# A spectral layer with an MLP behind it on one Trainium2 core: the second product two steps behind, eight places for the kept half, earlier reads, no preferred work

## Chip, cores and metric

The kernel runs on one core of a Trainium2 chip. The metric is the device time of one execution in microseconds (us), the median of several runs. All arrays are float32.

## What is computed

```
X  = rfft(x, axis=1)                       # x: 8 x 3008 x 256
Yr = Xr @ w_r - Xi @ w_i + b_r             # w_r, w_i: 256 x 256
Yi = Xr @ w_i + Xi @ w_r + b_i
Y  = sign(Y) * max(|Y| - 0.01, 0)          # real and imaginary part apart
y  = irfft(Y, n=3008, axis=1)
h  = y.reshape(24064, 256) @ w_in          # w_in: 256 x 2048, float64 in memory
out = max(0.01 * h, h) @ w_out             # w_out: 2048 x 256, float64 in memory
```

## The kernel before

Two pieces of work share TensorE. The **transform** of one batch element is cut as 3008 = 47 x 64: `fwd` (L229) does the 47-point stage, `mid` (L325) the 64-point stage (`stage_b`, L351), the projection (`proj`, L384), the threshold and the 64-point stage back (`stage_g`, L423), and `inverse` (L480) the 47-point stage back. The **MLP** goes over 32 chunks of 752 tokens. In `moe` (L639) a chunk has two phases.

- *Phase one* has eight steps, q = 0 to 7. A step makes 256 of the 2048 hidden features by seven block products in place of eight: `moe_a` (L553) issues four of them into the four `psh` banks, `moe_b` (L575 and the lines above it) three more onto three of these banks. Each product is three matmuls of 376 columns, since every operand is split into a high and a low part (`block`, L91, L98). Between the two groups VectorE and ScalarE must take sums out of the banks: L560 on ScalarE copies the first bank into `p1`, L561 to L563 on VectorE add the others. After the second group L575 and L577 (ScalarE, leaky ReLU) and L576 (VectorE) finish one token half, `gf`, and L580 (VectorE) with L584 (ScalarE) the other, `gs`, which is kept in SBUF until phase two. `parts` (L589) splits a half into its operands: `gh` by a copy on ScalarE (L594), `gl` by a subtraction on VectorE (L595). They rotate through six `gg` places, that is three pairs.
- The *second product*, `moe_o` (L602, matmuls on L612), adds a step's `gf` to two `pso` banks. In phase one it is issued in two groups of six matmuls, one behind `moe_a`, one behind `moe_b`, and takes the oldest entry of the list `behind`: the step before the present one.
- *Phase two* runs `moe_o` over the eight kept halves, 12 matmuls each. `late` (L598) splits a kept half; two are split in the last two steps of phase one, the others behind each group of phase two. `forms` (L508) makes the next chunk's operands meanwhile.

Transform work of the next batch element is traced between the groups. What order it gets is set by a scheduler: a list of ready instructions per engine, earliest traced first, with modelled times. `tc.issue_after` ties MLP matmuls to the order in which they are traced. `tc.high_priority(AHEAD)` (L560 to L563, L575 to L580) lets the instructions in it go ahead of up to 200 others.

The prologue (0 to about 145 us) reads and converts the weights and transforms the first batch element. `load_wout` (L192) reads w_out in eight pieces; the first `next(wout)` issues two of them behind `m0.finish()`. Two lines more are spoken of: the input tiles of the second batch element (`fwd(1)`) take the places that `XT` (L228) gives, the last pair that of `yc`, and `turns(0)` (L433) reads the first 64-point matrix.

Of the kernel before, what the change touches and what calls it, by code (L numbers as in the profile page):

```python
# [8 lines left out]
F32 = mybir.dt.float32  # L9
F32R = mybir.dt.float32r  # L10
U32 = mybir.dt.uint32
# [8 lines left out]
NG, NS = 5, 13  # L20
# [10 lines left out]
def spectral_mlp_kernel(  # L31
# [98 lines left out]
    def load_weights():  # L130

        w = early[:, 6 * D:6 * D + 3 * NH * D + P]
        r, d, n = (w[:, k * NH * D:(k + 1) * NH * D].rearrange("p (a f) -> p a f", a=NH) for k in range(3))
        i = sb.tile([P, NH, D], F32, name="w_i", tag="yt", bufs=1)
# [20 lines left out]
    made, converted, parted, early_parts = [], [], [], []  # L155
    AHEAD = 200

# [33 lines left out]
    def load_wout():  # L191
# [5 lines left out]
        def load():  # L197
            k = len(raws)
            raw = sb.tile([P, CS, 2], U32, name="raw", tag="ez"[k % 2], bufs=1)
            with tc.issue_after(reads[-1].ins):  # L200
                sync.dma_start(raw.rearrange("p (a f) w -> p a (f w)", a=n), ov[:, k * n:(k + 1) * n, :])
            raws.append(raw)
# [24 lines left out]
    NX = -(-NS // 2)  # L227
    XT = [("gs", NQ - 1)] * 2 + [("gg", 6)] * 3 + [("gs", NQ - 1), ("yc", 3)]  # L228

    def fwd(b):  # L230
# [5 lines left out]
        def load(c):  # L236
            cols = slice(2 * c * D, min(2 * c + 2, NS) * D)
            n = cols.stop - cols.start
            if b < NPRE:
                tag, bufs = XT[c]  # L240
                x_t[c] = [sb.tile([PA, 2 * D], F32, name="xin", tag=tag, bufs=bufs)[:, :n] for h in range(2)]
            else:
                x_t[c] = [
                    sb.tile([PA, 2 * D], F32, name=f"xin{h}", tag="uv"[h], bufs=3 - h)[:, :n] for h in range(2)
                ]
            for h, t in enumerate(x_t[c]):
                if b == 0:
# [76 lines left out]

    def mid(b):  # L325
        ud = u_dram[b]
        vd = dram.tile([2, NK1, NG * NS, D], F32, name="v_dram", tag="v_dram")
# [3 lines left out]
        act.dma_start(vd.rearrange("c k n d -> (c k) n d")[:, N2, :], zero)  # L331
        u_t, e_t, z_t, fb_t = {}, {}, {}, {}
        if b == 0:
# [4 lines left out]
        def load(j):  # L338
# [5 lines left out]
            u_t[j] = u  # L344

        def turns(j):
            if j < NPAIR:
                fb_t[j] = sb.tile([P, 3, N2], F32, name="fb", tag="fb")
                sync.dma_start(fb_t[j], fb[j])

# [27 lines left out]
        def proj(j):  # L378
# [4 lines left out]
            for dst, c, w in ((0, 2, "wr"), (0, 1, "wn"), (D, 0, "wd")):  # L383
# [5 lines left out]
                if c == 2:  # L389
                    kc = sb.tile([P, D], F32, name="kc", tag="kc", bufs=1)  # L390
# [8 lines left out]
            t = sb.tile([P, 2, D], F32, name="t", tag="t" if b else "v", bufs=1 if b else 2)  # L399
            c = sb.tile([P, 2, D], F32, name="c", tag="kb" if b else "yt", bufs=1)  # L400
            dve.tensor_add(flat(t), ps_y, flat(kb))  # L401
# [30 lines left out]

        turns(0)  # L433
        for j in range(2):
# [45 lines left out]
    def inverse(pi, eh):  # L480
# [11 lines left out]
        odd = sb.tile([P, 2 * NG * NK1], F32, name="odd", tag="odd", bufs=1)[:, :ne]  # L492
        y = sb.tile([P, CS], F32, name="y", tag="y")
        act.copy(odd, py[:, ne:2 * ne])
# [12 lines left out]
    def forms(ci):  # L507
# [3 lines left out]
        b11, b21, b12, b22 = y0[:, 0], y0[:, 1], y1[:, 0], y1[:, 1]  # L511
        t = sb.tile([P, 2, HT], F32, name="yt", tag="yt", bufs=1)
        y2 = sb.tile([P, 2, 7, 2, HP], F32R, name="yhl", tag="yhl", bufs=1)
# [11 lines left out]
        yield  # L525
        dve.tensor_sub(t[:, 1], b22, t[:, 0])
        dve.tensor_sub(b12, b22, b12)
        yield
        split(slice(2, 4), t)
        yield  # L530
        split(slice(4, 6), y1)
        dve.tensor_sub(b11, b21, t[:, 1])
        yield
# [15 lines left out]
    def moe_a(ci, q):  # L549
# [5 lines left out]
        product(c12, ci, q, 5, True)  # L555
        u = sb.tile([P, HT], F32, name="p1", tag="p1")
        g1 = sb.tile([P, 2, 2, HP], F32, name="gs", tag="gs", bufs=NQ - 1)
        g = g1[:, :, :, :HH]
        with tc.high_priority(AHEAD):
            act.copy(u, c11[:, :HT])  # L560
            dve.tensor_add(u, c22[:, :HT], u)  # L561
            dve.tensor_add(g[:, 1], halves(c21[:, :HT]), halves(u))  # L562
            dve.tensor_add(g[:, 1], halves(c12[:, :HT]), g[:, 1])  # L563
        h_t[ci, q] = (c11, c21, c12, u, g1)

    def moe_b(ci, q):
# [6 lines left out]
        g = g0[:, :, :, :HH]  # L573
        with tc.high_priority(AHEAD):
            act.activation(g[:, 0], halves(c11[:, :HT]), AF.Prelu, alpha=SLOPE)  # L575
            dve.tensor_add(g[:, 1], halves(c21[:, :HT]), halves(u))  # L576
            act.activation(g[:, 1], g[:, 1], AF.Prelu, alpha=SLOPE)  # L577
            parts(ci, q, 0, g0)
            g = g1[:, :, :, :HH]
            dve.tensor_add(g[:, 0], halves(c12[:, :HT]), halves(u))  # L580
        early_parts[:] = parted
# [57 lines left out]
    def moe():  # L639

        behind = []

        def next_o(eh):
            if behind:
                in_order(moe_o, *behind[0], eh)
                if eh:
                    behind.pop(0)

        for ci in range(nch):
            nxt = tokens(ci + 1) if ci + 1 < nch else iter(())  # L650
            units = 0
            for q in range(NQ):
# [8 lines left out]
                next(nxt, None)  # L661
                if q >= NQ - 2:
                    late(ci, q + 2 - NQ)
                units += 15
# [3 lines left out]
            nxt = forms(ci + 1) if ci + 1 < nch else iter(())  # L668
            behind += [(ci, q, 1) for q in range(NQ)]
            for q in range(NQ):  # L670
                for eh in range(NH):
                    next_o(eh)
                    if eh:
                        late(ci, q + 2)
                    with tc.issue_after(early_parts[0].ins), tc.issue_after(early_parts[1].ins):
# [3 lines left out]
        while behind:  # L679
            for eh in range(NH):  # L680
                next_o(eh)

# [27 lines left out]
    f0.to(0.01)  # L710
    load_win(0, (sync, act))
    load_weights()
    sign = const.tile([P, NK1 + NPAIR], F32, name="sign")
# [10 lines left out]
    with tc.issue_after(turned[0].ins):  # L724
        split_consts()
    m0 = Stream(mid(0), MID)
    m0.to(0.001)
# [12 lines left out]
    for i in range(1, 17):  # L740
# [3 lines left out]
        if 5 <= i < 12:  # L744
            next(fp.gen)
    m0.finish()
    fp.to(0.69)
    for p in due[0]:
        v_load(p)
    next(wout)  # L750
    for eh in range(NH):
# [143 lines left out]
```

## Time and profile before

| | |
|---|---|
| runs | 2581.2, 2583.67, 2587.37 us; median 2583.67 |
| profiled execution | 2589.46 us, its span 2587.7 us |
| TensorE (PE) busy / weight loads (PEld) busy | 2455.0 / 2336.0 us |
| VectorE (DVE) / ScalarE (ACT) / GpSimd (POOL) busy | 1891.2 / 1658.8 / 248.0 us |
| granted TensorE clock | 0.987 of 2.4 GHz |
| DMA | 173.68 MB, 67 GB/s on average |

The engines' queues run in order. A row of waits tells who stood idle, on which tile and line, and whose instruction ended the wait. In a timeline row the number in brackets is the idle time just before. "PE" rows are matmuls, whose ends are modelled, "PEld" rows weight loads, which run ahead of them. L-numbers are lines of the kernel before; in the order of the changed kernel they are those of the changed file.

### The profile page before, as it was taken

The numbers are of one execution on the slowest core, as the hardware profiler recorded it, in microseconds if no ns is written. First come the engines' busy times: TensorE is split into PE (matmuls) and PEld (weight loads), VectorE is DVE, ScalarE is ACT, GpSimd is POOL, SyncE is SP. The second block draws the span as 40 slices with busy tenths as digits, with TensorE's granted clock in tenths as the row PEclk, the third lists the DMA queues.
The fourth block names the chain that finished last, engine by engine and source line by source line (L and its number), as shares of the span: only waits on it lengthen the run. The fifth ranks groups of instructions, "written<-read, shape, count | busy, mean of one in ns | idle before, by whom it ended". The sixth has DMA issues, their size and how long they took to land.

```text
span 2587.7 us, 41422 instructions
## 1 busy us (share of the span) xinstructions
PE 2455.0 (95%) x15388; PEld 2336.0 (90%) x15388; DVE 1891.2 (73%) x3208; ACT 1658.8 (64%) x3198; POOL 248.0 (10%) x192
## 2 busy tenths in 40 slices
PE   6879999999999999999999999999999999999999
PEld 4569999999899998999989999899999999999998
DVE  6687788677776777777777767777768777766665
ACT  4666676667566666676656766566766666655554
POOL 0200012000110001100011001100002000000000
PEclk8989999999999999999999999999999999999999
DMA  7531123221231212321123211321213221100000
GB/s 234 164 119 54 49 56 114 71 57 51 71 95 53 57 45 76 86 66 49 49 81 86 57 53 44 93 79 51 60 50 100 65 59 40 44 28 28 17 13 19
DMA packets 138479, 173.68 MB, mean 67 GB/s; under 512 B 15661, under 2 KB 100645, under 8 KB 138277
## 3 DMA queue, kind: packets, MB, share of 16 engines
q1 hardware_dynamic: 97688, 124.17, 16.0%
q10 hardware_dynamic: 40589, 46.87, 7.1%
q8 instruction: 121, 1.98, 0.3%
q14 instruction: 81, 0.66, 0.1%
HBM read 95.22 MB, written 75.76 MB: 66 GB/s over the span
## 4 chain that ended last, share of the span: by engine, by line
PE 70%; DVE 12%; ACT 11%; DMA 3%; issue 2%; POOL 0%; SPq 0%; ACTq 0%; DVEq 0%; POOLq 0%
PE pso L612 30%; PE psh L98 25%; PE psf L82 10%; PE psf L491 3%; DVE gl L595 2%; ACT gh L594 2%; ACT zf L411 2%; PE psf L359 1%; ACT gf L577 1%; DVE t L403 1%; ACT zf L407 1%; DVE gs L562 1%; DVE t L401 1%; DVE p L561 1%; DVE gf L576 1%
## 5 line engine op out<-in xcount | busy, mean ns | idle before, releaser
L98 PE MATMUL psh<-yhl,win_hi 128*128 128x376 f32 x3584 | 884.0, 329 | 15.7 <-DVE gs L562 8.5
L98 PEld LDWEIGHTS psh<-yhl,win_hi 128*128 128x128 f32 x3584 | 610.8, 190 | 40.8 <-DVE gs L562 15.8
L98 PE MATMUL psh<-yhl,win_lo 128*128 128x376 f32 x1792 | 578.5, 323 | 0.0
L612 PE MATMUL pso<-gl,wout_hi 128*128 128x376 f32 x2048 | 505.1, 328 | 15.4 <-DVE gl L595 14.1
L612 PE MATMUL pso<-gh,wout_hi 128*128 128x376 f32 x2048 | 502.7, 327 | 15.4 <-ACT gh L594 15.2
L612 PE MATMUL pso<-gh,wout_lo 128*128 128x376 f32 x2048 | 496.7, 324 | 0.0
L612 PEld LDWEIGHTS pso<-gl,wout_hi 128*128 128x128 f32 x2048 | 353.0, 190 | 32.3 <-DVE gl L595 30.2
L612 PEld LDWEIGHTS pso<-gh,wout_hi 128*128 128x128 f32 x2048 | 353.6, 190 | 30.3 <-ACT gh L594 25.6
L612 PEld LDWEIGHTS pso<-gh,wout_lo 128*128 128x128 f32 x2048 | 359.1, 190 | 0.0
L98 PEld LDWEIGHTS psh<-yhl,win_lo 128*128 128x128 f32 x1792 | 339.0, 189 | 0.2 <-issue 0.2
L595 DVE TENSOR_TENSOR gl<-gf,gh 128x752 fp32r<-128x752 f32 x256 | 245.9, 961 | 106.8 <-ACT gh L594 104.5
L595 DVE TENSOR_TENSOR gl<-gs,gh 128x752 fp32r<-128x752 f32 x256 | 242.4, 958 | 63.8 <-ACT gh L594 63.6
L393 POOL TENSOR_TENSOR kb<-bias,kc 128x512 f32<-128x512 f32 x96 | 133.6, 1392 | 1613.5 <-ACT kc L391 1577.7
L594 ACT CAST gh<-gs 128x752 fp32r<-128x752 f32 x256 | 209.9, 822 | 111.4 <-PE pso L612 100.3
L575 ACT ACTIVATE gf<-psh 128x376 f32<-128x376 f32 x256 | 124.3, 485 | 234.0 <-PE psh L98 188.3
L561 DVE TENSOR_TENSOR p<-psh,p 128x376 f32<-128x376 f32 x256 | 140.1, 547 | 137.4 <-ACT p L560 121.4
L577 ACT ACTIVATE gf<-gf 128x376 f32<-128x376 f32 x256 | 132.6, 518 | 140.9 <-DVE gf L576 138.0
L576 DVE TENSOR_TENSOR gf<-psh,p 128x376 f32<-128x376 f32 x256 | 139.6, 545 | 112.7 <-PE psh L98 111.8
L594 ACT CAST gh<-gf 128x752 fp32r<-128x752 f32 x256 | 209.8, 820 | 6.2
L584 ACT ACTIVATE gs<-gs 128x752 f32<-128x752 f32 x256 | 212.1, 828 | 1.5 <-DVE gs L580 0.7
L560 ACT COPY p<-psh 128x376 f32<-128x376 f32 x256 | 117.8, 460 | 98.6 <-PE psh L98 98.4
L580 DVE TENSOR_TENSOR gs<-psh,p 128x376 f32<-128x376 f32 x256 | 139.5, 545 | 20.0 <-PE psh L98 17.7
(130 smaller groups left out, 3538.5 us busy)
## 6 DMA issues: line engine op xcount, KB each, us to landing
u<-u_dram SPq DMA_DIRECT2D x192, 128.0 KB, 2.8
v_dram<-v ACTq DMA_DIRECT2D x192, 128.0 KB, 2.4
out_dram<-ob SPq DMA_DIRECT2D x128, 188.0 KB, 1.9
vin<-v_dram SPq DMA_DIRECT2D x94, 240.0 KB, 3.4
xin<-x_dram SPq DMA_DIRECT2D x90, 240.0 KB, 3.0
u_dram<-xin ACTq DMA_DIRECT2D x72, 240.0 KB, 2.4
fb<-fb_dram SPq DMA_DIRECT2D x96, 96.0 KB, 2.0
u_dram<-xin SPq DMA_DIRECT2D x24, 240.0 KB, 3.9
```

What stands on the lines that cost most here:

```text
L82: last = nc.tensor.matmul(dst, a, b, start=(i == 0), stop=(i == len(terms) - 1))
L98: mlp[:] = [nc.tensor.matmul(dst, a, b, start=start and i == 0, stop=i == 2, skip_group_check=True)]
L393: pool.tensor_add(kb, bias, kc.unsqueeze(1).broadcast_to([P, 2, D]))
L561: dve.tensor_add(u, c22[:, :HT], u)
L575: act.activation(g[:, 0], halves(c11[:, :HT]), AF.Prelu, alpha=SLOPE)
L576: dve.tensor_add(g[:, 1], halves(c21[:, :HT]), halves(u))
L577: act.activation(g[:, 1], g[:, 1], AF.Prelu, alpha=SLOPE)
L580: dve.tensor_add(g[:, 0], halves(c12[:, :HT]), halves(u))
L584: act.activation(g, g, AF.Prelu, alpha=SLOPE)
L594: cp = act.copy(h, g)
L595: parted[:] = [cp, dve.tensor_sub(l, g, h.bitcast(F32))]
L612: mlp[:] = [nc.tensor.matmul(pv, a[:, f, s], turned_halves(r[:, i]), start=(f == 0 and j == 0), stop=(f == NF - 1 and j == 2),)]
```

## The change

Five edits, cut to the lines that matter:

```diff
 def moe():
-        def next_o(eh):
-            if behind:
+        def next_o(eh, least=2):
+            if len(behind) >= least:
                 in_order(moe_o, *behind[0], eh)
...
                 behind.append((ci, q, 0))
                 next(nxt, None)
-                if q >= NQ - 2:
-                    late(ci, q + 2 - NQ)
...
             behind += [(ci, q, 1) for q in range(NQ)]
+            late(ci, 0)
             for q in range(NQ):
                 for eh in range(NH):
                     next_o(eh)
                     if eh:
-                        late(ci, q + 2)
+                        late(ci, q + 1)
...
-        u = sb.tile([P, HT], F32, name="p1", tag="p1")
-        g1 = sb.tile([P, 2, 2, HP], F32, name="gs", tag="gs", bufs=NQ - 1)
+        u = sb.tile([P, HT], F32, name="p1", tag="p1", bufs=1)
+        g1 = sb.tile([P, 2, 2, HP], F32, name="gs", tag="gs", bufs=NQ)
-        with tc.high_priority(AHEAD):
-            act.copy(u, c11[:, :HT])
...
+        act.copy(u, c11[:, :HT])
...
-        with tc.high_priority(AHEAD):
-            act.activation(g[:, 0], halves(c11[:, :HT]), AF.Prelu, alpha=SLOPE)
-            dve.tensor_add(g[:, 1], halves(c21[:, :HT]), halves(u))
-            act.activation(g[:, 1], g[:, 1], AF.Prelu, alpha=SLOPE)
-            parts(ci, q, 0, g0)
-            g = g1[:, :, :, :HH]
-            dve.tensor_add(g[:, 0], halves(c12[:, :HT]), halves(u))
+        act.activation(g[:, 0], halves(c11[:, :HT]), AF.Prelu, alpha=SLOPE)
+        dve.tensor_add(g[:, 1], halves(c21[:, :HT]), halves(u))
+        act.activation(g[:, 1], g[:, 1], AF.Prelu, alpha=SLOPE)
+        g = g1[:, :, :, :HH]
+        dve.tensor_add(g[:, 0], halves(c12[:, :HT]), halves(u))
+        parts(ci, q, 0, g0)
...
 def forms(ci):
-        t = sb.tile([P, 2, HT], F32, name="yt", tag="yt", bufs=1)
+        t = sb.tile([P, 1, HT], F32, name="yt", tag="yt", bufs=1)
-        dve.tensor_sub(t[:, 1], b22, t[:, 0])
+        split(slice(2, 3), t)
...
-        split(slice(2, 4), t)
+        dve.tensor_sub(t[:, 0], b22, t[:, 0])
+        split(slice(4, 6), y1)
         yield
-        split(slice(4, 6), y1)
-        dve.tensor_sub(b11, b21, t[:, 1])
+        dve.tensor_sub(b11, b21, t[:, 0])
+        split(slice(3, 4), t)
...
 def load_wout():
             k = len(raws)
-            raw = sb.tile([P, CS, 2], U32, name="raw", tag="ez"[k % 2], bufs=1)
-            with tc.issue_after(reads[-1].ins):
+            if k < 2:
+                raw = early.bitcast(U32)[:, (13 + 4 * k) * D:(17 + 4 * k) * D].rearrange("p (f w) -> p f w", w=2)
+            else:
+                raw = sb.tile([P, CS, 2], U32, name="raw", tag="ez"[k % 2], bufs=1)
+            with tc.issue_after(reads[13 if k < 2 else -1].ins):
...
-    XT = [("gs", NQ - 1)] * 2 + [("gg", 6)] * 3 + [("gs", NQ - 1), ("yc", 3)]
+    XT = [("gs", NQ)] * 2 + [("gg", 6)] * 3 + [("gs", NQ), ("yc", 3)]
...
-                tag, bufs = XT[c]
+                tag, bufs = XT[c if c < NX - 1 else -1 - b]
...
     load_win(0, (sync, act))
+    m0 = Stream(mid(0), MID)
+    next(m0.gen)
     load_weights()
...
-    m0 = Stream(mid(0), MID)
     m0.to(0.001)
...
         if 5 <= i < 12:
             next(fp.gen)
+        if i == 13:
+            next(wout)
     m0.finish()
     fp.to(0.69)
     for p in due[0]:
         v_load(p)
-    next(wout)
```

`turns(0)` moves to the head of `mid`, so that the added `next(m0.gen)` issues that one read. Some scratch tiles change the place that they share (`w_i`, the threshold's `c` and `kc` of the first batch element, `y` at its own width), to make room for the eighth `gs`.

**Where phase one of a late chunk ends, on TensorE.** Before: `psh_26725` is the last group of step 7's `moe_b`, `gh_26697` and `gl_26698` are step 6's half and `gh_26763`, `gl_26764` step 7's, made from the three groups that end in the first two rows.

```order
L98 MATMUL psh_26725<-yhl_26158,win_hi_182 128x376 x2
L98 MATMUL psh_26725<-yhl_26158,win_lo_183 128x376
L612 MATMUL pso_26397<-gh_26697,wout_hi_920 128x376 x2
L612 MATMUL pso_26397<-gh_26697,wout_lo_921 128x376 x2
L612 MATMUL pso_26397<-gl_26698,wout_hi_920 128x376 x2
L612 MATMUL pso_26371<-gh_26763,wout_hi_920 128x376 x2
```

In the changed kernel `psh_26769` ends step 7's `moe_b`, `gh_26684` is step 5's half, `gh_26746` step 6's and `gh_26808` step 7's.

```order
L98 MATMUL psh_26769<-yhl_26197,win_hi_184 128x376 x2
L98 MATMUL psh_26769<-yhl_26197,win_lo_185 128x376
L616 MATMUL pso_26501<-gh_26684,wout_hi_920 128x376 x2
L616 MATMUL pso_26501<-gh_26684,wout_lo_921 128x376 x2
L616 MATMUL pso_26501<-gl_26685,wout_hi_920 128x376 x2
L616 MATMUL pso_26475<-gh_26746,wout_hi_920 128x376 x2
L616 MATMUL pso_26475<-gh_26746,wout_lo_921 128x376 x2
L616 MATMUL pso_26475<-gl_26747,wout_hi_920 128x376 x2
L616 MATMUL pso_26501<-gh_26746,wout_hi_920 128x376 x2
L616 MATMUL pso_26501<-gh_26746,wout_lo_921 128x376 x2
L616 MATMUL pso_26501<-gl_26747,wout_hi_920 128x376 x2
L616 MATMUL pso_26475<-gh_26808,wout_hi_920 128x376 x2
```

Between the last matmul of a step and the first use of what it made stood 6 matmuls; now 18 stand there.

**The last step of phase one of the chunk before that, on VectorE.** Before: the split of a kept half (`gl_26088`, from `gs_25696`) stands between the additions that empty the banks.

```order
L561 TENSOR_TENSOR p1_26107<-psh_26092,p1_26107 128x376
L595 TENSOR_TENSOR gl_26088<-gs_25696,gh_26087 128x4x188
L562 TENSOR_TENSOR gs_26108<-psh_26093,p1_26107 128x2x188
L563 TENSOR_TENSOR gs_26108<-psh_26094,gs_26108 128x2x188
L576 TENSOR_TENSOR gf_26128<-psh_26093,p1_26107 128x2x188
L580 TENSOR_TENSOR gs_26108<-psh_26094,p1_26107 128x2x188
```

In the changed kernel the first kept half that is split is `gs_25742`, in the last row.

```order
L566 TENSOR_TENSOR p1_26149<-psh_26134,p1_26149 128x376
L567 TENSOR_TENSOR gs_26150<-psh_26135,p1_26149 128x2x188
L568 TENSOR_TENSOR gs_26150<-psh_26136,gs_26150 128x2x188
L580 TENSOR_TENSOR gf_26170<-psh_26135,p1_26149 128x2x188
L583 TENSOR_TENSOR gs_26150<-psh_26136,p1_26149 128x2x188
L599 TENSOR_TENSOR gl_26176<-gf_26170,gh_26175 128x4x188
L528 TENSOR_TENSOR yt_26196<-yc_25905,yc_25453 128x376
L526 TENSOR_TENSOR yhl_26197<-yc_25453,yhl_26197 128x4x188
L532 TENSOR_TENSOR yc_25905<-yc_25905 128x376
L599 TENSOR_TENSOR gl_26187<-gs_25742,gh_26186 128x4x188
```

The split has moved behind the step's own work.

**The reads of w_out on SyncE's queue.** Before:

```order
L349 DMA fb<-fb_dram 128x192 x3
L475 DMA vin<-v_dram 120x512
L475 DMA early<-v_dram 120x512
L475 DMA vin<-v_dram 120x512
L475 DMA early<-v_dram 120x512
L294 DMA u_dram<-xin 120x512
L201 DMA raw<-w_out_dram 128x2x512
```

In the changed kernel:

```order
L333 DMA fb<-fb_dram 128x192
L203 DMA early<-w_out_dram 128x2x512
L333 DMA fb<-fb_dram 128x192
L203 DMA early<-w_out_dram 128x2x512
L333 DMA fb<-fb_dram 128x192
L480 DMA vin<-v_dram 120x512
L480 DMA early<-v_dram 120x512
L480 DMA vin<-v_dram 120x512
L480 DMA early<-v_dram 120x512
L203 DMA raw<-w_out_dram 128x2x512 x2
```

Two pieces of w_out are now read ahead of the `vin` reads, into a part of `early`, and two more right behind them.

## Rows read from the trace of the kernel before

**Rows 1.** The page, busy time by engine: us, share of the span, instructions.

```profile
PE 2455.0 (95%) x15388; PEld 2336.0 (90%) x15388; DVE 1891.2 (73%) x3208; ACT 1658.8 (64%) x3198; POOL 248.0 (10%) x192
```

**Rows 2.** Stretches: us, busy PE, PEld, DVE, ACT, POOL (count), clock, DMA share, GB/s.

```profile
0.00:145.00 145.00, 103.40 (x371) 67.65 (x372) 97.10 (x152) 80.48 (x158) 20.64 (x18) 0.87 0.67 197
...
195.00:2275.00 2080.00, 2007.52 (x12914) 1938.92 (x12913) 1540.79 (x2634) 1368.60 (x2663) 227.38 (x174) 0.99 0.23 64
2275.00:2535.00 260.00, 255.10 (x1591) 247.91 (x1590) 178.92 (x295) 151.90 (x275) 0.00 (x0) 1.00 0.07 23
```

**Rows 3.** Waits of PE, 195 to 2535 us: us in total, times, longest.

```profile
PE psf L82 <- ACT eh L374: 19.1, 15, 2.0
PE pso L612 <- ACT gh L594: 14.8, 34, 1.0
PE pso L612 <- DVE gl L595: 13.7, 27, 1.0
PE psf L82 <- ACT zh L418: 7.8, 6, 1.6
PE psh L98 <- DVE gs L562: 5.2, 11, 0.7
```

**Rows 4.** Waits of PEld, the weight loads, in the same stretch.

```profile
PEld pso L612 <- DVE gl L595: 29.2, 50, 1.2
PEld pso L612 <- ACT gh L594: 24.8, 35, 1.3
...
PEld psh L98 <- DVE gs L563: 12.4, 41, 0.6
PEld psh L98 <- DVE gs L562: 11.2, 23, 1.0
```

**Rows 5.** Timeline, end of phase one of a chunk: start us, us, engine.

```profile
2314.78 0.94 DVE L595 TENSOR_TENSOR gl<-gs,gh 128x752 fp32r<-128x752 f32 x1 [0.17 <-ACT gh L594]
...
2315.83 0.55 DVE L562 TENSOR_TENSOR gs<-psh,p 128x376 f32<-128x376 f32 x1
2316.43 0.59 PE L98 MATMUL psh<-yhl,win_hi 128*128 128x376 f32 x2 [0.71 <-DVE gs L562]
...
2317.99 0.48 PE L612 MATMUL pso<-gh,wout_lo 128*128 128x376 f32 x2
2318.31 0.48 PE L612 MATMUL pso<-gl,wout_hi 128*128 128x376 f32 x2
2318.35 0.82 ACT L594 CAST gh<-gf 128x752 fp32r<-128x752 f32 x1
...
2319.20 0.94 DVE L595 TENSOR_TENSOR gl<-gf,gh 128x752 fp32r<-128x752 f32 x1 [0.78 <-ACT gh L594]
2319.22 0.59 PE L612 MATMUL pso<-gh,wout_hi 128*128 128x376 f32 x2 [0.43 <-ACT gh L594]
2319.64 0.48 PE L612 MATMUL pso<-gh,wout_lo 128*128 128x376 f32 x2
```

**Rows 6.** Timeline, one step earlier: L580, and L560 of the next step.

```profile
2311.47 0.55 DVE L580 TENSOR_TENSOR gs<-psh,p 128x376 f32<-128x376 f32 x1
...
2313.58 0.45 ACT L560 COPY p<-psh 128x376 f32<-128x376 f32 x1
```

**Rows 7.** Chain of waits, 118 to 146 us: start us, us, what.

```profile
119.36 5.65 DMA raw<-w_out_dram
...
129.13 4.28 DMA raw<-w_out_dram
...
135.64 3.64 DMA u_dram<-xin
```

**Rows 8.** Timeline of PE, end of the prologue.

```profile
135.71 2.05 PE L491 MATMUL psf<-ga,early 120*128 120x128 f32 x8 [4.01 <-ACT xin L293]
140.51 3.74 PE L82 MATMUL psf<-xin,fa 120*120 120x512 f32 x4 [2.75 <-DVE y L497]
```

**Rows 9.** Costs by line: the operands' split in `forms` that is cut in two.

```profile
L520 ACT CAST yhl<-yt 128x752 fp32r<-128x752 f32 x32 | 26.6, 831 | 2.9 <-DVE yt L526 2.9
```

More of the change, by code (lines that the diff above doesn't have):

```diff
@@ L133, in load_weights @@
         r, d, n = (w[:, k * NH * D:(k + 1) * NH * D].rearrange("p (a f) -> p a f", a=NH) for k in range(3))
-        i = sb.tile([P, NH, D], F32, name="w_i", tag="yt", bufs=1)
+        i = sb.tile([P, NH, D], F32, name="w_i", tag="t", bufs=1)
         for t, src in ((r, w_r), (i, w_i)):
@@ L155, in spectral_mlp_kernel @@
     made, converted, parted, early_parts = [], [], [], []
-    AHEAD = 200
     NIN = DF // 4
@@ L325, in mid, with turns @@
     def mid(b):
+        u_t, e_t, z_t, fb_t = {}, {}, {}, {}
+        def turns(j):
+            if j < NPAIR:
+                fb_t[j] = sb.tile([P, 3, N2], F32, name="fb", tag="fb")
+                sync.dma_start(fb_t[j], fb[j])
+        turns(0)
+        if b == 0:
+            yield 0
         ud = u_dram[b]
@@ L331, in mid @@
         act.dma_start(vd.rearrange("c k n d -> (c k) n d")[:, N2, :], zero)
-        u_t, e_t, z_t, fb_t = {}, {}, {}, {}
         if b == 0:
@@ L344, in load @@
             u_t[j] = u
[L346 to L349, printed above, removed]
         def stage_b(j):
@@ L389, in proj @@
                 if c == 2:
-                    kc = sb.tile([P, D], F32, name="kc", tag="kc", bufs=1)
+                    kc = sb.tile([P, D], F32, name="kc", tag="kc" if b or j % 2 else "p1", bufs=1)
                     act.copy(kc, ps_k[:, :D])
@@ L399, in proj @@
             t = sb.tile([P, 2, D], F32, name="t", tag="t" if b else "v", bufs=1 if b else 2)
-            c = sb.tile([P, 2, D], F32, name="c", tag="kb" if b else "yt", bufs=1)
+            c = sb.tile([P, 2, D], F32, name="c", tag="kb" if b else "t", bufs=1)
             dve.tensor_add(flat(t), ps_y, flat(kb))
@@ L431, in stage_g @@
                 act.dma_start(vd[c, 2 * j:2 * j + 2, :N2, :].rearrange("k n d -> n k d"), v[c * N2:(c + 1) * N2])
-        turns(0)
         for j in range(2):
@@ L492, in inverse @@
         odd = sb.tile([P, 2 * NG * NK1], F32, name="odd", tag="odd", bufs=1)[:, :ne]
-        y = sb.tile([P, CS], F32, name="y", tag="y")
+        y = sb.tile([P, 2 * NG * N1], F32, name="y", tag="y")
         act.copy(odd, py[:, ne:2 * ne])
@@ L555, in moe_a @@
         product(c12, ci, q, 5, True)
-        u = sb.tile([P, HT], F32, name="p1", tag="p1")
-        g1 = sb.tile([P, 2, 2, HP], F32, name="gs", tag="gs", bufs=NQ - 1)
+        u = sb.tile([P, HT], F32, name="p1", tag="p1", bufs=1)
+        g1 = sb.tile([P, 2, 2, HP], F32, name="gs", tag="gs", bufs=NQ)
         g = g1[:, :, :, :HH]
-        with tc.high_priority(AHEAD):
-            act.copy(u, c11[:, :HT])
-            dve.tensor_add(u, c22[:, :HT], u)
-            dve.tensor_add(g[:, 1], halves(c21[:, :HT]), halves(u))
-            dve.tensor_add(g[:, 1], halves(c12[:, :HT]), g[:, 1])
+        act.copy(u, c11[:, :HT])
+        dve.tensor_add(u, c22[:, :HT], u)
+        dve.tensor_add(g[:, 1], halves(c21[:, :HT]), halves(u))
+        dve.tensor_add(g[:, 1], halves(c12[:, :HT]), g[:, 1])
         h_t[ci, q] = (c11, c21, c12, u, g1)
@@ L573, in moe_b @@
         g = g0[:, :, :, :HH]
-        with tc.high_priority(AHEAD):
-            act.activation(g[:, 0], halves(c11[:, :HT]), AF.Prelu, alpha=SLOPE)
-            dve.tensor_add(g[:, 1], halves(c21[:, :HT]), halves(u))
-            act.activation(g[:, 1], g[:, 1], AF.Prelu, alpha=SLOPE)
-            parts(ci, q, 0, g0)
-            g = g1[:, :, :, :HH]
-            dve.tensor_add(g[:, 0], halves(c12[:, :HT]), halves(u))
+        act.activation(g[:, 0], halves(c11[:, :HT]), AF.Prelu, alpha=SLOPE)
+        dve.tensor_add(g[:, 1], halves(c21[:, :HT]), halves(u))
+        act.activation(g[:, 1], g[:, 1], AF.Prelu, alpha=SLOPE)
+        g = g1[:, :, :, :HH]
+        dve.tensor_add(g[:, 0], halves(c12[:, :HT]), halves(u))
+        parts(ci, q, 0, g0)
         early_parts[:] = parted
@@ L680, in moe @@
             for eh in range(NH):
-                next_o(eh)
+                next_o(eh, 1)
     class Stream:
```

## Prediction

> **What bounds the kernel now.** The page comes first: TensorE (PE) is busy 95% of the span, VectorE 73%, ScalarE 64% [rows 1]. So PE is the engine to watch, and the others matter where PE waits for them. The stretches come next [rows 2]. The prologue is the worst: PE works 103.4 of 145 us, at a clock of 0.87. In the long stretch with transform and MLP it leaves 72.5 of 2080 us idle, in the MLP alone 4.9 of 260. Together that is 77.4 us of plain idle time. The weight loads leave more: 141.1 and 12.1 us, 153.2 in all.
>
> The waits say who PE stood still for [rows 3]. The two largest concern the second product: 28.5 us in 61 stalls for its operands, 14.8 for `gh` from ScalarE and 13.7 for `gl` from VectorE. The others are the transform's operands (19.1 and 7.8) and the sums that VectorE takes out of the `psh` banks. The weight loads' waits show the same places, larger [rows 4]: 54.0 us for the second product, 23.6 for `psh`.
>
> A stall costs more than its idle time. In [rows 5] an undisturbed pair of matmuls takes 0.32 us (2317.99 to 2318.31). From 2318.31 to 2319.64 pass 1.33 us for two pairs that need 0.64: 0.69 us lost, where the row shows 0.43 idle. The other 0.26 us is the refilling of the pipe. The Trainium skill (Perfetto Trace Analysis, Identifying the Most-Contended Engine) calls the busy share of matmuls a poor measure of what is left and that of weight loads a good one. The rows agree with it: by PE's idle time alone the whole loss behind the prologue would be 77 us, by the loads 153.
>
> **The second product's operands.** Present cost: 28.5 us idle and 61 times 0.26 make 44.4; the loads' waits say 54.0, since some stalls are too short to leave PE idle. I take 50. How late are the operands? In [rows 5] the last step's groups are followed from 2317.67 (one pair ahead of 2317.99) by the second product. `gh` is done at 2319.17 (2318.35 and 0.82), 1.50 us later; `gl` at 2320.14 (2319.20 and 0.94), 2.47 us later. Before, 6 matmuls stood between, 0.96 us; now 18, 2.88 us, and `gl` is used four matmuls behind `gh`, 3.5 us. Both are covered with 1.0 us or more to spare. Inside phase one a `gl` had 18 matmuls and those four, 3.5 us, against the same 2.47; that margin of 1.0 us was used up wherever another row stood ahead on ScalarE or VectorE. A whole step of 33 matmuls, 5.3 us, is added. In phase two the shortest distance, in either order, between the last use of a pair of `gg` places and the first use of the half that fills it next rises from 14 matmuls to 26 (2.2 to 4.1 us), against 1.76 us for one copy and one subtraction. So nearly all goes: **-45**. Ends: -25 if only phase one's half goes, -54 if all.
>
> **The sums out of the banks.** Two things change. The kept halves that were split in the last two steps of phase one now wait for phase two. [Rows 5] shows what that split did: 0.94 us of VectorE at 2314.78, behind it L562 only at 2315.83, and PE idle 0.71 us at 2316.43 for just this addition. There are two such splits in each of 32 chunks. And the preference is gone; yet in the changed order 151 of 256 steps have the three additions L566 to L568 in one piece, where before it was 89. The loads' waits here are 23.6 us [rows 4]. I take half: **-12**. Ends: 0 and -24.
>
> **The transform's waits.** Its operands stop PE for 26.9 us in 21 stalls [rows 3], with refilling 32. They now compete on equal terms. The shortest distance in the order from a transform bank to the first use of its operand `eh` goes from 12 matmuls (nine of 84 cases) to 15; for `zh` from 3.4 to 6.8 us of matmul work. These are small steps: **-10**. Ends: +5 (a stall more in one case of four) and -25.
>
> **What comes back.** PE will run closer together, and everything that ran beside it has less time. VectorE is busy 74% of the long stretch and ScalarE 66% [rows 2]; over a stretch 60 us shorter that is 76 and 68, so neither becomes the bound. But a sum that was just in time behind a stall is late without it. I let a quarter of these 67 us return: **+17**. Ends: 0, and the whole (first rival).
>
> **Prologue.** The chain waits 5.65 and 4.28 us for w_out and 3.64 us for a write of `xin` whose place `yc` needs [rows 7]; PE itself stands 4.01 and 2.75 us [rows 8]. The first two reads of w_out now stand on SyncE's queue ahead of the `vin` reads, and `xin` of the second element no longer sits in a `yc` place. PE's two stalls are the price nearest to the end: **-7**. Ends: -13.6, the whole of the chain's waits, and +1.4: two conversion copies, each less than the 0.82 of a 752-column copy in [rows 5], now stand on ScalarE inside the first element's transform, where PE waits for it. The moved reads wait until VectorE is through with their part of `early`, which the conversion of w_in uses; behind them on SyncE stand one `fb` read each and the `vin` reads, and these need the transform's last writes anyway. The read of the first matrix (`turns(0)`) goes one place ahead of w_r on the same queue; the product waits there for `u`, so nothing.
>
> **At no cost.** In `forms` one split of 752 columns becomes two of 376: 32 copies of 0.83 us [rows 9] become 64 of about 0.45 [rows 6], and likewise on VectorE; even at 0.55 each that is 8.6 us on an engine that is idle a third of the time, and the result is wanted only by the next chunk's first product. If that cover is gone, 8.6 us is the price. One place for `p1`: the copy L560 of a step must now wait for the preceding L580. In [rows 6] L580 ends at 2312.02 and L560 starts at 2313.58, 1.56 us to spare. The eighth `gs` frees a wait that is not in the lists.
>
> **Sum.** -45 - 12 - 10 + 17 - 7 = -57 us. From the profiled execution's 2589.46 that is 2532.5. This execution stands 5.8 us above the median of the runs, 2583.67, so the forecast is 2526.7, rounded **2527**.
>
> **Rivals.**
> - *The waits only move.* PE reaches the `psh` banks sooner and waits there for L562 and L563, which stand three matmuls apart. For it: 64 waits of the loads there now, the second largest place [rows 4]. Against it: the additions stand closer together in the order. If all 67 us but a quarter return (+50 in place of +17), -24 is left, and with no gain in the prologue -17: 2567. Chance 0.17, a third of it within 0.2% of before.
> - *The places are the limit.* The second product's operands still rotate through six `gg` places. If phase two's stalls come from these, half of the first term stays: -57 and 25, less a quarter: 2546. The Trainium skill (Perfetto Trace Analysis, Optimization Strategy) says that the same gap coming back on the busiest engine can mean too few buffers; by it the six places, which stay, would be the cause. The distance of 26 matmuls in place of 14 speaks against it. Chance 0.08.
> - *Slower: late L583, one `p1`.* Without preference a transform row stands ahead of L583 in 135 of 256 steps of the changed order, against 77 before. Such a row takes between 0.55 and 0.94 us (the additions and the split in [rows 5]); take 0.75. A late L583 now holds up the next L565, which starts the sums, and PE stops at the second group of `moe_b`. If each of the 135 steps loses 0.75 us, that is 101 us against a gain of 57: 2628. It decides once L583 is over 1.56 us later than in [rows 6]; a loss of 0.42 us a step makes the change slower. One row does not use up the margin, two would. Chance 0.09.
>
> **How the numbers follow.** The forecast's own case, 2485 to 2555, has 0.66. A measurement of this kernel can tell about 0.2% (5 us) from no change. Faster by more: 0.66, 0.08 and two thirds of 0.17: 0.85. Within: 0.06. Slower: 0.09. All terms at their better ends with nothing returned would be -117 us, 2467; all of that together is unlikely, so the range starts at 2484 and reaches past the first rival, to 2576. What is left out: the slower case, the last of the first rival, and a twentieth below.
>
> **What would show it.** Right: in 195 to about 2480 us the waits of the loads for `gh` and `gl` fall from 54 to under 10 us; the loads idle under 105 us in place of 153; the waits for L567 and L568 together fall to some 12 us; ScalarE's wait for w_out is gone from the chain ahead of 145 us. Wrong: these waits fall and those on `psh` or on the transform's operands rise by as much (first rival); `gl` waits of over 20 us stay in phase two (second); ScalarE's L565 waits for VectorE's L583 (third).

## The result, and the profile after

The changed kernel takes **2538.27 us** (median of 4 runs, 2534.03 to 2538.79), the kernel before in the same comparison 2583.27 us: a ratio of 0.982, 95% interval 0.9803 to 0.9837, or 45 us less. The forecast was 2527, its range 2484 to 2576. The profiled execution took 2538.32 us with a span of 2536.2; against the profiled execution of before it is 51.1 us shorter, since that one stood 5.8 us above its median and this one at it.

First the page's busy times and the stretches, as in [rows 1, 2]. What ran near 2275 us before runs near 2225 now, so the cuts lie there (columns as in rows 2).

```profile
PE 2432.7 (96%) x15388; PEld 2341.0 (92%) x15388; DVE 1869.1 (74%) x3240; ACT 1654.2 (65%) x3230; POOL 245.3 (10%) x192
```

```profile
0.00:145.00 145.00, 108.10 (x403) 70.87 (x404) 103.13 (x167) 83.74 (x165) 22.37 (x18) 0.91 0.67 198
...
195.00:2225.00 2030.00, 1976.59 (x12819) 1931.57 (x12819) 1513.55 (x2647) 1358.07 (x2680) 222.92 (x174) 0.99 0.23 65
2225.00:2484.00 259.00, 257.25 (x1634) 254.46 (x1633) 181.59 (x302) 154.34 (x282) 0.00 (x0) 1.00 0.08 24
```

The loads' idle time, 2030 less 1931.57 and 259 less 254.46, is 103.0 us, against 153.2. PE's own is 55.2 against 77.4. From the first MLP product to the end of the span passed 2444.4 us before and 2401.5 now, 43 less. The Trainium skill (Perfetto Trace Analysis, Identifying the Most-Contended Engine) holds the loads to be the better measure of what is left; the rows agree again: they gave 50 back, PE's idle time only 22.

The waits tell where, PE's and then the weight loads', 195 to 2484 us (us in total, times, longest). They answer to [rows 3] and [rows 4].

```profile
PE pso L616 <- ACT ob L622: 35.6, 30, 3.3
PE psh L98 <- DVE gs L567: 10.2, 19, 0.8
PE psf L82 <- ACT eh L380: 5.9, 12, 0.6
...
PE psf L82 <- ACT zh L424: 0.5, 1, 0.5
```

```profile
PEld pso L616 <- ACT ob L622: 45.5, 36, 3.6
PEld psh L98 <- DVE gs L567: 17.2, 27, 1.0
PEld psf L82 <- ACT eh L380: 11.1, 17, 0.9
PEld psh L98 <- DVE gs L568: 5.1, 24, 0.3
PEld psh L98 <- ACT p L565: 2.9, 6, 0.8
```

No line for `gh` or `gl` is left: 54.0 us are gone. At the head of both lists stands a wait that had cost the loads 2.4 us before, and that the prediction never named (the last row below, 195 to 2535 us): for `ob`, the copy (L622) by which ScalarE empties a `pso` bank so that the kept half's groups may write there.

```profile
PEld pso L612 <- ACT ob L618: 2.4, 11, 0.3
```

The timeline of one turn from the first token half to the second shows it (start us, us, engine; idle time in brackets).

```profile
1135.61 0.48 PE L616 MATMUL pso<-gl,wout_hi 128*128 128x376 f32 x2
1136.12 0.50 ACT L525 CAST yhl<-yt 128x376 fp32r<-128x376 f32 x1
1136.53 0.37 ACT L376 COPY xi<-psf 128x256 f32<-128x256 f32 x1
...
1136.79 0.59 ACT L377 CAST eh<-psf 128x512 fp32r<-128x512 f32 x1
...
1137.27 0.83 ACT L598 CAST gh<-gs 128x752 fp32r<-128x752 f32 x1
...
1137.99 0.83 ACT L525 CAST yhl<-yc 128x752 fp32r<-128x752 f32 x1
...
1138.71 0.48 ACT L622 COPY ob<-pso 128x376 f32<-128x376 f32 x1
...
1139.24 0.59 PE L616 MATMUL pso<-gh,wout_hi 128*128 128x376 f32 x2 [3.15 <-ACT ob L622]
```

The first bank was full near 1135.1, for the six matmuls on the second bank, which end in the first row, start at 1134.97; a copy of 0.48 us would have been done in time. It starts at 1138.71, because ScalarE, whose queue runs in order, works through the next chunk's operands (`yhl`), a kept half's split and the transform's rows first, without a pause. Not every turn is like this one. Of the 30 stalls of PE for `ob` nine, of 1.97 to 3.34 us, make 25.1 of the 35.6 us; the four behind 2225 us, where the 64-point stage of the transform is over, take 0.43 to 0.44 each.

The prologue, on PE: the row of before and the row now in which the first MLP product starts, 8.5 us apart.

```profile
143.26 1.18 PE L98 MATMUL psh<-yhl,win_hi 128*128 128x376 f32 x1
```

```profile
133.10 1.95 PE L82 MATMUL psf<-xin,fa 120*120 120x512 f32 x4 [0.93 <-ACT yhl L525]
134.74 0.47 PE L98 MATMUL psh<-yhl,win_hi 128*128 128x376 f32 x1
```

Of the stalls of 4.01 and 2.75 us ahead of it [rows 8] one of 0.93 remains. The start varies between kernels with the same prologue: in the nine traces that keep all of this edit it lies between 134.74 and 137.16, in the three without it between 141.91 and 144.07.

### The profile page after: what moved, and what is told of

It is laid out like the page before. It is cut to its first block, busy times and chain, and to the rows that moved or that the text cites. A ratio compares the mean times of both kernels' runs of the same rounds, so it can differ in the third digit from the quotient of the medians.

```text
span 2536.2 us, 41553 instructions
## 1 busy us (share of the span) xinstructions
PE 2432.7 (96%) x15388; PEld 2341.0 (92%) x15388; DVE 1869.1 (74%) x3240; ACT 1654.2 (65%) x3230; POOL 245.3 (10%) x192
## 4 chain that ended last, share of the span: by engine, by line
PE 75%; ACT 11%; DVE 3%; issue 2%; DMA 0%; POOL 0%; ACTq 0%; DVEq 0%; SPq 0%
PE pso L616 32%; PE psh L98 28%; PE psf L82 10%; PE psf L496 3%; ACT gh L598 3%; PE psf L365 2%; ACT yhl L525 2%; ACT zf L417 1%; ACT gs L588 1%; ACT gf L581 1%; ACT zf L413 1%; DVE t L407 1%; DVE gf L580 1%; ACT ob L622 1%; ACT eh L377 0%
## 5 line engine op out<-in xcount | busy, mean ns | idle before, releaser
L616 PE MATMUL pso<-gh,wout_hi 128*128 128x376 f32 x2048 | 506.4, 329 | 35.6 <-ACT ob L622 35.6
L616 PEld LDWEIGHTS pso<-gh,wout_hi 128*128 128x128 f32 x2048 | 358.8, 192 | 46.5 <-ACT ob L622 45.8
L616 PEld LDWEIGHTS pso<-gl,wout_hi 128*128 128x128 f32 x2048 | 359.9, 191 | 0.8
L580 DVE TENSOR_TENSOR gf<-psh,p 128x376 f32<-128x376 f32 x256 | 139.8, 546 | 99.5 <-PE psh L98 98.8
L568 DVE TENSOR_TENSOR gs<-psh,gs 128x376 f32<-128x376 f32 x256 | 140.3, 548 | 22.2 <-PE psh L98 3.4
L567 DVE TENSOR_TENSOR gs<-psh,p 128x376 f32<-128x376 f32 x256 | 140.2, 548 | 19.9 <-PE psh L98 1.5
```

Of the source, the lines that this page charges most:

```text
L616: mlp[:] = [nc.tensor.matmul(pv, a[:, f, s], turned_halves(r[:, i]), start=(f == 0 and j == 0), stop=(f == NF - 1 and j == 2),)]
```

## The experiments

Each was timed in five rounds against the kernel before, which took 2584.5 to 2585.9 us (medians) beside them; beside the change it took 2583.3. So a difference of under some 3 us between two rows says nothing.

| kernel | median us | ratio to before (95%) |
|---|---|---|
| the change | 2538.3 | 0.982 (0.9803 to 0.9837) |
| lag undone | 2579.1 | 0.9974 (0.9965 to 0.9984) |
| splits moved, lag undone | 2597.1 | 1.0045 (1.0031 to 1.0059) |
| preferred again | 2548.3 | 0.986 (0.9842 to 0.9878) |
| prologue undone | 2544.0 | 0.984 (0.9827 to 0.9854) |
| first `ob` on VectorE | 2537.6 | 0.9815 (0.9802 to 0.9828) |
| forms held back | 2496.1 | 0.9661 (0.9648 to 0.9674) |
| in pairs | 2517.2 | 0.974 (0.9727 to 0.9753) |
| **both of these** | **2484.5** | 0.9615 (0.9602 to 0.9628) |
| held back, lag undone | 2565.5 | 0.9922 (0.9909 to 0.9935) |
| before, no preference | 2584.3 | 1.000 (0.9991 to 1.0009) |
| before, one `p1` | 2582.5 | 0.9993 (0.9984 to 1.0002) |

### What the distance is worth

**Lag undone.** The changed kernel with the second product and the splits of the kept halves as before:

```diff
-        def next_o(eh, least=2):
+        def next_o(eh, least=1):
...
+                if q >= NQ - 2:
+                    late(ci, q + 2 - NQ)
...
-            late(ci, 0)
...
-                        late(ci, q + 1)
+                        late(ci, q + 2)
```

> The second product again one step behind and two kept halves split in the last two steps of phase one; eight places, no preference and the earlier reads stay. Theory (the distance took the gh and gl waits away, and moving the two splits into phase two is what made the output copy late): the weight loads' waits for gh and gl come back to 40 to 60 us, their wait for the output copy ob falls from 45 to under 15 us, time 2555 to 2580 us. Rival (the missing preference or the eighth place took them away): gh and gl waits stay under 15 us and the time stays within 8 us of the changed kernel's 2538.

The time came out at the edge of the theory, 2579.1. The loads' waits, 195 to 2484 us:

```profile
PEld psh L98 <- DVE gs L567: 18.2, 34, 0.8
PEld psf L82 <- ACT eh L380: 16.4, 22, 1.9
PEld pso L616 <- ACT gh L598: 14.9, 22, 1.5
PEld pso L616 <- ACT ob L622: 14.4, 29, 3.5
PEld psh L98 <- DVE gs L568: 14.1, 51, 0.7
PEld pso L616 <- DVE gl L599: 11.0, 25, 0.9
```

`gh` and `gl` are back, but with 25.9 us and not 40 to 60; the sums rose (32.3, in the change 22.3), and most of the rest came at the transform's banks, `psf`: 60.3 us of the loads' waits, against 17.3 in the change and 56.2 before. Before, the largest of them were these (195 to 2535 us), which [rows 4] does not show:

```profile
PEld psf L82 <- ACT eh L374: 24.4, 20, 2.2
PEld psf L82 <- ACT zh L418: 9.5, 6, 1.9
PEld psf L82 <- DVE xz L268: 7.1, 11, 1.2
```

In time all but 6 us of the gain is gone, about what the prologue's edits are worth (below). So the gain of the steady part hangs on the lag and the splits that move with it.

**Splits moved, lag undone** takes the two apart: `least=1`, everything else as in the change.

> The changed kernel, but the second product goes one step behind again; all kept halves are still split in phase two. Theory (distance in phase one and at its end took away some 39 of the 54 us of gh and gl waits, and the splits moved to phase two bring the wait for the output copy): gh and gl waits of the loads 20 to 40 us, the wait for ob still over 20 us, time 2570 to 2595 us. Rival (moving the splits is what gained, the longer distance in phase one is worth little): 2535 to 2550 us with gh and gl under 10.

```profile
PEld pso L616 <- DVE gl L599: 46.2, 75, 2.9
PEld pso L616 <- ACT gh L598: 22.7, 33, 1.4
PEld pso L616 <- ACT ob L622: 12.8, 19, 3.5
PEld psf L82 <- ACT eh L380: 9.8, 14, 1.9
PEld psf L82 <- ACT zh L424: 8.4, 6, 1.7
```

2597.1 is slower than before and 2 us over the theory's range: moving the splits alone loses 18 us against the kernel with the lag undone. Much of that is how this one order happens to fall. Five times PE stands 2.56 us for a `gl` whose subtraction takes 2.00 us in place of 0.94 while GpSimd works:

```profile
1014.55 2.00 DVE L599 TENSOR_TENSOR gl<-gs,gh 128x752 fp32r<-128x752 f32 x1
...
1016.61 0.59 PE L616 MATMUL pso<-gl,wout_hi 128*128 128x376 f32 x2 [2.56 <-DVE gl L599]
```

`gh` and `gl` cost more than expected (68.9) and `ob` less (12.8). It is less than with the splits where they were (14.4), so moving them is not what makes `ob` late as long as the distance is short; that PE's standing for `gl` gives the copy its time fits both runs, but was not tested apart. Nor was the longer distance with the splits left in place.

The longer distance, with the splits moved, is worth 2597.1 - 2538.3 = 59 us. Not all of it is the second product's operands. From 195 us to the end of the span the loads' waits in this run exceed the change's by 63 us: `gh` and `gl` by 71.5 and the transform's banks by 36.4, while `ob` has 31.9 less and `psh` 13.1 less. The transform's share hangs on the distance in every kernel of the study: with the second product two steps behind, the loads' waits at `psf` are 10 to 26 us, with one step 54 to 60. How the distance does that was not tried apart.

**Preferred again**, the change with both `tc.high_priority` blocks back, and **before, no preference**, the kernel before without them:

```diff
-        act.copy(u, c11[:, :HT])
...
+        with tc.high_priority(200):
+            act.copy(u, c11[:, :HT])
```

> The changed kernel with the preference for the sums out of the psh banks back on ScalarE and VectorE. Theory (the preference decides little): time 2530 to 2546 us, the loads' waits for psh between 18 and 28 us as without it. Rival A (preferred sums would take the psh waits away and leave the rest): psh waits under 8 us, time 2515 to 2530. Rival B (the preference starves the transform's evictions): waits for eh, zh and xz of the loads go from 17 back to over 30 us, time 2548 to 2560.

> The kernel before, with nothing but the two preferences taken out. Putting the preference back into the changed kernel cost 10 us. Theory (the preference costs the same in both, by putting sums ahead of what PE waits for sooner): 2570 to 2578 us. Rival (it costs only beside the longer distance): 2580 to 2588 us, and the gh and gl waits of the loads keep their 53 us.

In the kernel before the preference decides nothing (1.000). In the changed one it costs 10 us (8 when each kernel is set against the one before beside it). That is the time of the second rival, but not its mechanism: the loads' waits are hardly others (`ob` 47.2, the first addition into `gs` 16.6, `eh` 10.5); only 5.3 us in which PE waits for reads of `u` from DRAM stand out. The profiled execution is the fastest of the four, 2544.3 us; the other three ran at a mean clock of 0.982 to 0.984 against its 0.987. Where the 10 us come from is left open. The psh waits are the same with and without: they do not hang on the preference. In the kernel before without it the loads keep 52.6 us of `gh` and `gl` waits (195 to 2430 us).

**Prologue undone**: the two early reads of w_out and the place of the second element's last input pair put back.

```diff
-            if k < 2:
-                raw = early.bitcast(U32)[:, (13 + 4 * k) * D:(17 + 4 * k) * D].rearrange("p (f w) -> p f w", w=2)
-            else:
-                raw = sb.tile([P, CS, 2], U32, name="raw", tag="ez"[k % 2], bufs=1)
-            with tc.issue_after(reads[13 if k < 2 else -1].ins):
+            raw = sb.tile([P, CS, 2], U32, name="raw", tag="ez"[k % 2], bufs=1)
+            with tc.issue_after(reads[-1].ins):
...
-                tag, bufs = XT[c if c < NX - 1 else -1 - b]
+                tag, bufs = XT[c]
...
-        if i == 13:
-            next(wout)
```

> The changed kernel with w_out's first two reads behind the vin reads and the second element's last input pair in the yc places again. Theory (the prologue's edits gave the 8.5 us by which the first MLP matmul moved): time 2544 to 2549 us, first MLP matmul near 143 us. Rival (the prologue's gain was swallowed later, since the first elements' transform sets the pace there): within 3 us of 2538.

2544.0, 5.8 us over the change, or 3.8 when each is set against the kernel before beside it; the intervals of the two ratios overlap, so the size is uncertain. The first MLP product started at 138.32 and not near 143, so part of the 8.5 us comes from other moved places and reads that this run left in.

**Before, one `p1`**: `bufs=1` on that tile and nothing else.

> The kernel before with one place for p1 in place of two and nothing else. Theory (L580 has been done for over a microsecond when the next step copies into p1): 2579 to 2590 us, no change that can be told, ScalarE's copy into p1 waits for no addition. Rival (the slower case of the prediction, which would also explain why the psh waits did not fall in the changed kernel): psh waits of the loads over 30 us in place of 22, time over 2592.

No difference (0.9993). ScalarE's one wait for L580 ahead of its copy into `p1`, 195 to 2484 us:

```profile
ACT p L560 <- DVE gs L580: 1.8, 1, 1.8
```

One wait in 256 steps: the margin of 1.56 us [rows 6] holds.

### What the new wait is made of

**First `ob` on VectorE.**

```diff
-            act.copy(ob, po)
+            (act.copy if eh else dve.tensor_copy)(ob, po)
```

> The changed kernel, but the copy that empties the first of the two pso banks runs on VectorE instead of ScalarE (the second stays). Theory (TensorE stands 35.6 us, 30 times, because that copy is queued on ScalarE behind the splits of the next operands): this wait falls under 8 us and the time to 2490 to 2510 us. Rival (the wait only moves, to the split of the first kept half, to VectorE's queue or to the second bank): the wait stays over 20 us in sum under other names, time 2525 to 2540.

The theory in its simple form fell: 2537.6, no gain. PE's waits, 195 to 2484 us:

```profile
PE pso L616 <- DVE ob L622: 15.9, 24, 1.4
PE pso L616 <- ACT ob L622: 14.9, 7, 2.2
```

VectorE's queue holds the low parts of the same splits, each behind its copy on ScalarE, so its `ob` is late too; and the second bank's copy, still on ScalarE, stops PE six matmuls later. So it does not help to move this one row; the next two runs ask whether it is all that ScalarE has to do at the turn.

**Forms held back.** The next chunk's operands wait until both output copies are issued:

```diff
-            act.copy(ob, po)
+            outs.append(act.copy(ob, po))
...
-                    with tc.issue_after(early_parts[0].ins), tc.issue_after(early_parts[1].ins):
-                        next(nxt, None)
+                    if q >= 2:
+                        with tc.issue_after(outs[-2].ins), tc.issue_after(outs[-1].ins):
+                            next(nxt, None)
```

> The changed kernel, but the next chunk's operands (forms) are held back until both output copies of the first half are issued, which takes three yhl copies (0.83, 0.52 and 0.83 us, 2.2 us together) from ahead of them on ScalarE; the splits of the kept halves and the transform's rows stay ahead. Theory (it is the burst on ScalarE at the turn of the halves that makes the copy late): the loads' wait for ob falls from 45 to between 8 and 25 us, time 2505 to 2522 us. Rival (as when VectorE took the first copy: the wait goes to another name at the turn): the loads' waits at pso stay over 35 us in sum, time 2530 to 2542.

2496.1: 42 us less than the change, for moving the rows of `forms`, on ScalarE and VectorE, behind two copies. The loads' waits, 195 to 2430 us, the long stretch, and the page's busy times:

```profile
PEld psh L98 <- DVE gs L567: 19.2, 31, 1.0
PEld pso L616 <- ACT ob L622: 17.9, 30, 1.8
```

```profile
195.00:2225.00 2030.00, 1999.17 (x13081) 1953.85 (x13080) 1527.04 (x2692) 1381.98 (x2727) 240.80 (x174) 1.00 0.24 66
```

```profile
PE 2416.0 (97%) x15388; PEld 2323.8 (93%) x15388; DVE 1855.7 (74%) x3240; ACT 1656.1 (66%) x3230; POOL 265.0 (11%) x192
```

The wait for `ob` fell by 27.6 us, as expected; `gh` and `gl` cost 5.1, and all waits in the loads' list together fell from 88 to 64. The time fell by 42, more than the theory had. The missing 18 are busy time: the same 15388 matmuls take PE 2416.0 us in place of 2432.7, 16.7 less. The clock accounts for about that: its mean over the span rises from 0.987 to 0.993, and 0.6% of 2500 us is 15, an estimate from these two figures (see the last section).

**In pairs**: the first four halves of phase two go two and two, both on the first bank and then both on the second.

```diff
+            row = []
+            for q in range(0, NQ, 2):
+                two = [behind.pop(0), behind.pop(0)]
+                row += [(k, eh) for eh in range(NH) for k in two] if q < 4 else [(k, eh) for k in two for eh in range(NH)]
-            for q in range(NQ):
-                for eh in range(NH):
-                    next_o(eh)
+            for n, (k, eh) in enumerate(row):
+                for q in (n // 2,):
+                    in_order(moe_o, *k, eh)
...
-                        late(ci, q + 1)
+                        late(ci, len([1 for _, e in row[:n + 1] if e]))
```

> The changed kernel, but the first four halves of phase two go in pairs, both groups on the first pso bank and then both on the second, so that 12 matmuls (1.9 us) in place of 6 (0.96 us) stand between the last use of a bank and its next. Theory (the handover is short of time, on whichever engine the copy runs): some 0.96 us less for each of the 31 turns that stall, the loads' wait for ob 15 to 25 us, time 2510 to 2525. Rival (what the turn gains is lost at the second kept half, whose pair of gg places is now free only 12 matmuls ahead of its use, against 0.83 and 0.93 us of splitting): gh and gl waits of the loads come back to over 15 us, time 2532 to 2545.

2517.2, the middle of the theory: the loads (195 to 2430 us) wait 18.0 us for `ob`, 15 times, and 5.6 for `gh` and `gl` together, so the second kept half is nearly always ready. The Trainium skill (Perfetto Trace Analysis, Optimizing Tensor Performance) wants independent groups of matmuls to rotate through different PSUM banks so that one is emptied beside the next group. The groups here do rotate, through two banks, and it was not enough: six matmuls, 0.96 us, were shorter than ScalarE's queue at that point, and doubling them gave 21 us.

**Both.**

> Both of the last two edits: the operands held back and the first four halves in pairs. Theory: the loads' wait for ob under 8 us, time 2495 to 2512. Rival (the psh sums or the transform become late instead): waits at psf and psh grow from 40 to over 60 us, time over 2520.

2484.5, the best kernel of the study, 54 us below the change and 100 below before; the loads' waits for `ob` are 6.0 us, the sums of `psh` 23.9 and the largest that is left.

**Held back, lag undone**: forms held back and `least=1`.

> The same with the next chunk's operands held back behind the output copies, which gave 42 us beside the longer distance. Theory (the two are apart: the hold takes the burst away from ScalarE, the distance covers the last steps' operands): 2530 to 2560 us, gh and gl waits of the loads 15 to 40 us, ob under 15. Rival (the hold alone does it, the distance is no longer needed): within 8 us of 2496.

2565.5, 5 us over the theory's upper end, with 56.8 us of `gh` and `gl` waits (expected up to 40) and 3.5 for `ob`. The rival, that the hold makes the distance needless, is out by 69 us. With the turn cleared the distance is worth 69, without it 59. Here too the transform's banks are late again, with 59.9 us of the loads' waits against 10.3 with the hold and the longer distance.

## Why the prediction was right, and where not

The time lay in the range and the direction was right; the sum, -57, missed by 6 us in the profiled executions (-51.1) and by 12 in the medians. But the terms are further off than the sum: their errors cancel, and that the sum came so near is in good part luck.

- **The second product's operands, -45 (ends -25 and -54).** The better end: 54.0 us of waits of the loads are gone. The margins worked out from [rows 5] held everywhere, in phase two as well. The run that undoes the distance alone brings these waits back, 68.9 us of them; its 59 us of time also hold what the distance does to the transform's waits and to `ob`.
- **The sums out of the banks, -12.** Failed: 23.6 us before, 22.3 now for the same two additions (17.2 and 5.1), and 2.9 more for L565. Two steps were wrong. "There are two such splits in each of 32 chunks" took the row at 2314.78 for a pattern; in the whole trace of before a split of a kept half stood ahead of L562 in a stall of the loads of over half a microsecond six times, five of them behind 2275 us. And additions that stand in one piece in the order are not early for that. In the changed kernel it is a transform's row that stands between them:

```profile
1118.71 0.55 DVE L566 TENSOR_TENSOR p<-psh,p 128x376 f32<-128x376 f32 x1 [2.03 <-ACT p L565]
...
1119.18 0.40 DVE L500 TENSOR_TENSOR y<-psf,odd 128x240 f32<-128x240 f32 x1
...
1119.49 0.39 DVE L502 TENSOR_TENSOR y<-psf,odd 128x230 f32<-128x230 f32 x1
...
1119.80 0.54 DVE L567 TENSOR_TENSOR gs<-psh,p 128x376 f32<-128x376 f32 x1
...
1120.39 0.59 PE L98 MATMUL psh<-yhl,win_hi 128*128 128x376 f32 x2 [0.76 <-DVE gs L567]
```

  This stall comes back with each batch element at the same place (814.57, 1120.39, 1426.06, 1736.07, 2042.20).
- **The transform's waits, -10 (ends +5 and -25).** Undersized, and for the wrong reason. PE's waits for `eh` and `zh` alone fell from 26.9 us [rows 3] to 6.4, and the loads' at all `psf` banks from 56.2 to 17.3. For the other two terms the prediction went by the loads' list, for this one by PE's; in the loads' list the transform's banks stood level with the second product and `psh` was third, not "the second largest place". Nor is it the equal terms that the prediction named: with the preference back `eh` stays at 10.5 us for the loads, and in the kernel before without it at 24.5. The small steps in the order were a poor measure as well. What the waits follow is the second product's distance: in the three runs that undo it they are back at 54 to 60 us. By which path is open.
- **What comes back, +17, "a sum that was just in time".** The size and the place failed: 43.1 us came back (45.5 for `ob` against 2.4), at the `pso` banks and not at `psh`. The prediction followed each moved split to the next use of its `gg` place and never asked what else ScalarE has to do at the turn. A kept half's split, the first pieces of `forms` and in the long stalls the transform's rows fall on the 0.96 us that a bank has between its two groups. That PE's standing for `gl` at the turn had hidden this before is argued, not shown. That ScalarE at 66% does not become "the bound" is said of an average; at the turn it is another number (columns as in rows 2):

```profile
1130.00:1136.00 6.00, 6.00 (x41) 5.80 (x39) 5.71 (x10) 5.13 (x9) 0.00 (x0) 1.00 0.06 18
1136.00:1140.50 4.50, 1.35 (x9) 1.26 (x9) 3.81 (x7) 4.48 (x11) 0.00 (x0) 1.00 0.29 92
```

  4.48 of 4.5 us on ScalarE while PE works 1.35. The split of `forms` was costed at nothing for the same reason; holding those rows back gave 42 us, so their place, not their length, was the price.
- **Prologue, -7.** Near, as far as it can be told: 8.5 us at the first MLP product, and 4 to 6 in the time by the run that undoes the reads and the place, with intervals that overlap.
- **At no cost: one `p1`.** Right: nothing changes in the kernel before, and in the changed one ScalarE's waits ahead of L565 name TensorE alone.

*The rivals.* "The waits only move" had the mechanism, a wait that takes the place of one removed, but named `psh`, where the sum of the loads' waits stood still: the first addition's rose by 6.0 us, the second's fell by 7.3, and 2.9 came for L565. "The places are the limit" is out: six `gg` places stand, and no `gl` wait is left. "Slower: late L583" is out by the changed kernel itself, which is faster and has no wait of L565 for L583; the run with one `p1` kept the preference, so it tests only half of this rival.

*What would show it.* The `gh` and `gl` waits under 10 us (none) and the loads idle under 105 us (103.0) were as written; the waits for L567 and L568 at 12 us were not (22.3). The chain of after is not followed back to the prologue, so the sign for w_out can't be read from it; ScalarE still waits 4.35 us for that read at 123.24, but PE no longer stands still for it.

## What to carry to other kernels

A consumer that waits for its operands at every turn is cured by issuing it later, but a stall also gives time to everything else that is due at that turn: list what each engine must do between the last use of a bank or place and its next, and compare that sum, not the engine's mean share, with the matmuls that stand there. Where it is too long, first move the rows that are wanted late (here the next chunk's operands) behind the copy that frees the bank, and then put more matmuls between the two uses; the two together were worth 54 us here, more than the change itself.

## What was not expected of the hardware

A long stall can cost more than its idle time and the 0.26 us that the prediction counts beside it. In the stretch from 1136.00 to 1140.50 (the second windows row of the section on the prediction) PE stood 3.15 us for `ob`. In the next stretch the granted clock is 0.52 of full speed, close to the lower of the two levels (1.2 of 2.4 GHz), though PE is busy throughout; the timeline shows the pairs.

```profile
1140.50:1144.00 3.50, 3.50 (x13) 3.50 (x12) 3.50 (x7) 2.13 (x4) 0.00 (x0) 0.52 0.18 67
```

```profile
1140.62 0.81 PE L616 MATMUL pso<-gh,wout_lo 128*128 128x376 f32 x2
1141.22 0.83 PE L616 MATMUL pso<-gl,wout_hi 128*128 128x376 f32 x2
...
1143.73 0.64 PE L616 MATMUL pso<-gh,wout_hi 128*128 128x376 f32 x2
1144.21 0.48 PE L616 MATMUL pso<-gh,wout_lo 128*128 128x376 f32 x2
```

From 1140.62 to 1144.21 six pairs take 3.59 us in place of 1.92: 1.67 us lost behind a wait of 3.15, and as busy time, so that no list of waits shows it. Between 195 and 2484 us the trace of the change has ten such stretches with a granted clock of 0.50. Nine of them begin in or right behind the nine longest stalls of PE for `ob` (1.97 to 3.34 us), the tenth, at 1546.9, behind three short stalls in a row (0.48, 0.49 and 0.35 us). With the longest wait of the loads for `ob` down to 1.8 us (forms held back) no such stretch is left: the long stretch runs at a mean clock of 1.00 in place of 0.99.
